# Softmax denominators: seven tiles summed onto the same 224 columns, and the logarithm read from that bank

## The chip, the cores and the metric

The kernel runs on one core of one Trainium2 chip. The metric is the device time in microseconds (us) of one execution; a figure for a kernel is the median of its runs.

## The reference, cut to what matters

Inputs are q, k and v of shape 8 x 12 x 448 x 64 (batch, heads, sequence, head width), two gains of 64, and the weights w_in (768 x 2048) and w_out (2048 x 768) of a two-layer network.

```python
q_n, k_n = rmsnorm(q, g_q), rmsnorm(k, g_k)
scores = scale * q_n @ k_n.transpose(0, 1, 3, 2)
attn = exp(scores - max)
attn = attn / (sum(attn, axis=-1) + 1e-09)     # the sum is the denominator of this case
x = (attn @ v) reshaped to (8 * 448, 768)
h = x @ w_in
out = maximum(0.01 * h, h) @ w_out             # leaky relu between the two products
```

## The kernel before

**Units.** The attention is cut into 24 units, numbered u = 0 to 23. A unit is four heads of one batch element, held as two pairs: index `a` picks the pair and index `r` the head of the pair (`r` is the upper or lower half of the 128 partitions of the scores). The 448 sequence positions are seven tiles of 64 (`NS` = 7). Three units make one batch element, and each batch element then passes through the two-layer network, whose pieces stand in a queue.

**One unit.** For each of the seven key tiles TensorE makes the scores (`score`, L195) into a slot: two banks of PSUM, the tile `sT`. ScalarE writes `et` = exp(score + shift) in 16 bits (`ex`, L214). The shift comes from the first tile: VectorE takes its maximum (L232) and spreads it on a diagonal (L234), TensorE transposes it (`shift_mm`, L244), VectorE reduces it again (L245) and makes the bias `eb` (L253). There are two slots, so the scores of the coming tiles wait until the exponentials of earlier ones have read their slot.

**Close of a unit.** When the scores of the first tile of unit u have been issued (step d = 0 of four), unit u-1 is closed. For units 4 to 22 (`narrow`) this is done as follows, in this order:

- `pv_slot`: 28 matmuls (L341) give exp times v in the other slot, without the division; each is a 64 x 64 piece of TensorE, and four of them run beside each other.
- `zcol`: the sums of exp, the denominators, go to a bank `zc` (L283). The stationary operand `onesr` has 32 columns of ones and zeros, so that each matmul uses 128 rows and 32 columns of the array. Four such matmuls, for the four combinations of the half `y` of the sequence and the pair `a`, use the four strips of 32 columns beside each other. The kernel before takes two key tiles in one matmul where it can: three groups of 448 columns (two tiles side by side) and one group of 224 columns (the seventh tile, added onto the first half). That makes 16 matmuls, and the bank then holds two halves of 224 columns.
- `shift_mm` for unit u, then `pv_out` (ScalarE copies the undivided result from the slot to `x32`, L295).
- `zcol_sum`: VectorE adds the two halves of `zc` into `zs` (L300), after which the bank can be used again.

Then the exponential of unit u's first tile is issued. Later, as a job between the pieces of the network, `zcol_inv` takes on ScalarE exp(-ln(zs)) (L305 and L306) and issues four DMAs on SP's queue that spread the reciprocals over the partitions (`rz`, L311). A later step on GpSimd or VectorE multiplies `x32` by `rz` into `xt` (L321), the input of the network.

**The order of the work.** All order is written by hand in the loop at L928 to L1006. `fill` takes pieces of the network out of the queue and puts one waiting job after each piece. `moe1` is six matmuls of 448 columns (`hps`, L363) and the leaky relu on ScalarE (L357). `moe2` and `seven` are the second product (L404, L445). In the last batch elements `late1` gives the first product in other pieces (L565, with L575 and L578 behind them).

**Banks.** PSUM has two slots of two banks and four further banks in rotation, called `aux`. `zc`, `hps` and the accumulators of the second product come out of these four, so that the fourth request after `zc` gets the bank of `zc`. From the late pieces on the four banks stand in a list (`held`): `aux` takes the first and `drop` appends.

For the last unit, u = 23, the job `zcol_inv` of unit 22 is issued at step d = 1 and not at d = 0.

Of the kernel before, what the change touches and what calls it, by code (L numbers as in the profile page):

```python
# [10 lines left out]
AF = mybir.ActivationFunctionType  # L11
ALU = mybir.AluOpType
AXL = mybir.AxisListType
# [5 lines left out]
def kernel(  # L19
# [11 lines left out]
    nc = tc.nc  # L31

    B, H, S, D = q.shape
    QH = 4
    NS = 7
# [21 lines left out]
    def aux(shape, dtype, name):  # L57
        if held:
            return held[0].pop(0)
        return psum.tile(shape, dtype, tag="aux", bufs=4, name=name)  # L60
# [6 lines left out]
    def drop(bank):  # L67
        if held:
            held[0].append(bank)
# [5 lines left out]
    onesr = cst.tile([P, 32], FP16)  # L75
# [47 lines left out]
    def load_v(u):  # L123
        nc.gpsimd.dma_start(vts[u % NV].rearrange("p a t d -> p a (t d)"), rows(v, u))  # L124
# [73 lines left out]
    def qk(u, steps):  # L198
        st[u]["sT"] = []
        for t in steps:  # L200
            sT = slot()
            score(u, t, (sT[:, 0], sT[:, 1]))
            st[u]["sT"].append((t, sT))

    def ex(u):
        s = st[u]
        if "et" not in s:
            s["et"] = epool.tile([P, NS, 2, S], FP16, tag="et", name="et")
        for t, sT in s["sT"]:
            if isinstance(sT, list):  # L210
                for a in range(2):
                    nc.scalar.activation(s["et"][:, t, a], sT[a][:, 0:S], AF.Exp, bias=s["eb"], scale=1.0)
            else:
                nc.scalar.activation(s["et"][:, t], sT[:, :, 0:S], AF.Exp, bias=s["eb"], scale=1.0)  # L214
# [6 lines left out]
    def shift_max(u):  # L221
        s = st[u]
        sT = s["sT"][0][1]
        if isinstance(sT, list):
            pm2 = small.tile([P, 2], FP32, tag="pm2", name="pm2")
            for a in range(2):
                nc.vector.tensor_reduce(pm2[:, a:a + 1], sT[a][:, 0:S], axis=AXL.X, op=ALU.max)
            s["spare"] = sT[0]
            nc.vector.tensor_reduce(s["spare"][:, 511:512], pm2, axis=AXL.X, op=ALU.max)
        else:  # L230
            s["spare"] = sT[:, 0]
            nc.vector.tensor_reduce(s["spare"][:, 511:512], sT[:, :, 0:S], axis=AXL.XY, op=ALU.max)  # L232
        s["dg"] = small.tile([P, P], FP16, tag="dg", name="dg")
        nc.vector.tensor_tensor(s["dg"], ident16, s["spare"][:, 511:512].broadcast_to([P, P]), op=ALU.mult)  # L234
# [20 lines left out]
    def gate(u):  # L255
        nc.gpsimd.tensor_copy(gate_t, buf(u, "n16")[:, 1, NS - 1, 1, D - 1:D])
# [11 lines left out]
    def zsum_slot(u):  # L268
        s = st[u]
        s["zslot"] = slot()  # L270
        s["zt"] = [s["zslot"][:, r] for r in range(2)]
        zsum(u)

    HS = S // 2

    def zcol(u):
        s = st[u]
        s["zc"] = aux([P, 512], FP32, "zc")
        for i, (t, n) in enumerate(((0, 2), (NS - 1, 1), (2, 2), (4, 2))):
            for y in range(2):  # L280
                for a in range(2):
                    c = 32 * (2 * y + a)
                    nc.tensor.matmul(s["zc"][c:c + 32, 0:n * HS].rearrange("p (k x) -> p k x", k=n), onesr,  # L283
                                     s["et"][:, t:t + n, a, HS * y:HS * y + HS], start=(i == 0), stop=(i == 3))

    def pv_slot(u):
        s = st[u]
        s["pslot"] = slot()
        s["pv"] = [s["pslot"][:, r] for r in range(2)]
        pv(u)  # L290

    def pv_out(u):
        s = st[u]
        s["x32"] = zpool.tile([P, 2, S], FP32, tag="x32", name="x32")
        nc.scalar.copy(s["x32"], s["pslot"][:, :, 0:S])  # L295

    def zcol_sum(u):
        s = st[u]
        s["zs"] = zpool.tile([P, HS], FP32, tag="zs", name="zs")
        nc.vector.tensor_reduce(s["zs"], s["zc"][:, 0:S].rearrange("p (k x) -> p x k", k=2), axis=AXL.X, op=ALU.add)  # L300
        drop(s["zc"])

    def zcol_inv(u):
        s = st[u]
        nc.scalar.activation(s["zs"], s["zs"], AF.Ln)  # L305
        nc.scalar.activation(s["zs"], s["zs"], AF.Exp, bias=0.0, scale=-1.0)  # L306
        s["rz"] = zpool.tile([P, 2, S], FP32, tag="rz", name="rz")
        for r in range(2):
            for y in range(2):
                src = s["zs"][64 * y + r:64 * y + 64:2, None, :]  # L310
                nc.sync.dma_start(s["rz"][:, r, HS * y:HS * y + HS], src.broadcast_to([32, 4, HS]))  # L311

    def xmul_sb(u):
        xmul_pool(u, nc.vector)
# [382 lines left out]
    def narrow(u):  # L697
        return 4 <= u < NU - 1

    def fed(u, d):  # L700
        return u % NQ == 0 and d == 3
# [43 lines left out]
    with tc.manual_schedule():  # L745
# [182 lines left out]
        for u in range(3, NU):  # L928
            for d in range(4):
                if d > 0 or u > 3:  # L930
                    qk(u, STEPS[d])
                    if d == 0:
                        shift_max(u)
                        if u == 6:
                            xmul_sb(u - 2)
                        if narrow(u - 1):
                            pv_slot(u - 1)
                            zcol(u - 1)
                            shift_mm(u)
                            pv_out(u - 1)  # L940
                            zcol_sum(u - 1)
                        else:
                            zsum_slot(u - 1)
                            pv(u - 1)
                            shift_mm(u)
                            zinv(u - 1)
                    ex(u)
                jobs = []

                def job(fn, *args):  # L950
                    jobs.append(lambda: fn(*args))

                if d == 0:
                    if u == 3:
                        prep_norm(4)
                        gate(4)
                    elif narrow(u - 1):
                        if u < NU - 1:
                            job(zcol_inv, u - 1)
                    else:  # L960
                        xmul(u - 1)
                    if u + 4 < NU:
                        job(load, u + 4)
                    if u + 3 < NU:
                        load_v(u + 3)
                    if u < 6:
                        prep_sqp(u + 3)
                if d == 1 and narrow(u - 1) and not 5 <= u < 8 and u < NU - 1:
                    xmul_pool(u - 1)
                if u == NU - 1:  # L970
                    if d == 1:
                        job(zcol_inv, u - 1)
                    if d == 2:
                        xmul_pool(u - 1)
                if fed(u, d) and u > 3:
                    push(u // NQ - 1)
                if (u, d) in ((3, 1), (4, 0)):
                    for ti in range(2):
                        prep_tr(u + 1, ti, VV)
                if d == 1 and 5 <= u < NU - 1:  # L980
                    job(prep_g, u + 1)
                if u + 2 < NU:
                    if d == 1:
                        for ti in range(2):
                            job(prep_ssq, u + 2, ALL, (ti,))
                    if d == 2:
                        job(prep_rinv, u + 2)
                        for ti in range(2):
                            job(prep_norm, u + 2, ALL, (ti,))
                        if u > 3:  # L990
                            job(prep_trd, u + 2)
                if d == 1 and 4 <= u < 8:
                    job(weight_sum, u - 4, 0)
                if d == 0 and 5 <= u < 9:
                    job(weight_sum, u - 5, 1)
                if d == 2 and 6 <= u < 8:
                    job(xmul_sb, u - 1)
                if u == NU - 2 and d == 0:
                    for n, tile_ in ((1, (raws, "rq", 3)), (2, (raws, "rk", 3)), (3, None), (4, (prep_p, "sq", 3))):
                        job(win_sum, n, 1, tile_)  # L1000
                    for n in (3, 1, 2, 4):
                        job(x_sum, LATE, n)
                if d == 3 and 6 <= u < NU - 3:
                    for ti in range(2):
                        job(prep_sq, u + 3, ALL, (ti,))
                fill(u, d, jobs)  # L1006
# [4 lines left out]
        for i, ns in enumerate(((3, 1), (2, 4))):  # L1011
            c, fn = queue[i]
# [33 lines left out]
```

## Time and profile before

| What | Value |
|---|---|
| Median of 5 runs | 421.41 us (420.49 to 423.85) |
| Time of the profiled execution | 422.01 us |
| Its span, first to last instruction | 420.2 us |
| Around the span | 1.81 us |
| Mean granted TensorE clock | 0.990 of full speed |
| TensorE, matmuls (PE) | 404.6 us busy, 96% of the span |
| TensorE, weight loads (PEld) | 217.8 us, 52% |
| VectorE (DVE) | 279.9 us, 67% |
| ScalarE (ACT) | 304.8 us, 73% |
| GpSimd (POOL) | 82.9 us, 20% |
| `zc` matmuls L283, 19 units | 304 matmuls |
| `zs` sum on VectorE L300 | 19 instructions, 622 to 624 ns each |
| ln L305 and exp L306 on ScalarE | 19 each, 395 and 390 ns |

PE is TensorE's matmuls and PEld its weight loads, which lie beside the matmuls. A matmul's duration in the profile contains its way through the array, so that neighbouring matmuls overlap; how long a row of matmuls holds TensorE is read from the distance of their starts, or from the chain of waits.

### The profile page before, as it was taken

How to read it: one execution, taken by the hardware profiler on the slowest of the kernel's cores; microseconds unless marked ns; L12 is line 12 of the kernel's file. 1: busy time of each engine (PE TensorE's matmuls, PEld its weight loads, DVE VectorE, ACT ScalarE, POOL GpSimd, SP SyncE). 2: the span in 40 equal slices, each digit the busy share in tenths (PEclk: the TensorE clock that was granted, in tenths of full speed). 3: DMA queues.
4: the chain of work that ended last, by engine and by line, in shares of the span. 5: the costliest groups of instructions: out<-in, count | busy, mean ns of one | idle time of the engine just before them, and what ended most of it. 6: DMA issues, size and time to landing. Idle time of an engine off the chain costs nothing.

```text
span 420.2 us, 9148 instructions
## 1 busy us (share of the span) xinstructions
PE 404.6 (96%) x3731; PEld 217.8 (52%) x3731; DVE 279.9 (67%) x459; ACT 304.8 (73%) x474; POOL 82.9 (20%) x75
## 2 busy tenths in 40 slices
PE   7977999999999999999999999999999999999995
PEld 6544444444445544454445544454445547558853
DVE  5788666898569746567349856478349888627762
ACT  5999878867987779867986779967986757653600
POOL 0958421300020111220111112121101101010000
PEclk9699999999999999999999999999999999999999
DMA  7999995989664796687565797577562460032023
GB/s 255 219 251 257 239 250 111 194 156 213 172 153 73 217 211 118 171 159 175 157 125 118 194 192 161 144 143 192 162 112 45 119 148 17 2 83 76 2 53 98
DMA packets 71949, 62.39 MB, mean 148 GB/s; under 512 B 36324, under 2 KB 67044, under 8 KB 71908
## 3 DMA queue, kind: packets, MB, share of 16 engines
q1 hardware_dynamic: 61312, 49.62, 46.6%
q0 software_dynamic: 10272, 11.80, 17.9%
q8 instruction: 29, 0.48, 0.4%
q10 hardware_dynamic: 324, 0.39, 0.3%
q14 instruction: 12, 0.10, 0.1%
HBM read 45.61 MB, written 11.01 MB: 135 GB/s over the span
## 4 chain that ended last, share of the span: by engine, by line
PE 82%; ACT 8%; DVE 6%; issue 1%; DMA 1%; SPq 0%; DVEq 0%; ACTq 0%
PE hps L363 27%; PE sT L195 8%; PE sT L341 6%; PE ma L445 5%; PE md L445 5%; PE mc L445 5%; ACT et L214 5%; PE bank L445 5%; PE bank L565 4%; PE op L404 3%; PE zc L283 3%; PE mb L445 3%; DVE n L167 2%; PE sT L445 2%; DMA rk<-in_k_dram 1%
## 5 line engine op out<-in xcount | busy, mean ns | idle before, releaser
L214 ACT ACTIVATE et<-sT,eb 128x896 f16<-128x896 f32 x166 | 159.5, 1009 | 17.9 <-PE sT L195 16.3
L363 PE MATMUL hps<-xt,win 128*128 128x448 f16 x600 | 120.8, 353 | 0.2 <-DVE xt L350 0.2
L363 PEld LDWEIGHTS <-win 128*128 128x128 f16 x612 | 56.8, 98 | 58.2 <-issue 9.6
L321 POOL TENSOR_TENSOR xt<-x,rz 128x896 f16<-128x896 f32 x16 | 33.2, 2076 | 148.7 <-DMA rz<-zs 117.8
L167 DVE TENSOR_TENSOR n<-rq,rinv 128x896 f16<-128x896 f32 (+2 forms) x25 | 26.8, 1075 | 51.5 <-ACT rinv L161 48.7
L357 ACT ACTIVATE gt<-hps 128x448 f16<-128x448 f32 x100 | 52.4, 549 | 5.4 <-PE hps L363 5.1
L195 PE MATMUL sT<-qkT 64*64 64x448 f16 x664 | 53.2, 368 | 3.0 <-ACT et L214 2.1
L155 DVE TENSOR_REDUCE ssq<-sq 128x14 f32<-128x896 f32 (+2 forms) x49 | 50.4, 1058 | 1.7 <-ACT sq L144 1.7
L445 PEld LDWEIGHTS <-sa 128*128 128x128 f16 x352 | 32.8, 98 | 26.3 <-issue 6.1
L295 ACT COPY x<-sT 128x896 f32<-128x896 f32 x19 | 17.2, 906 | 36.1 <-DVE sT L245 36.1
L124 POOL DMA_DIRECT2D vt<-in_v_dram x24 | 18.2, 758 | 114.4 <-PE sT L341 106.9
L445 PEld LDWEIGHTS <-gt 128*128 128x128 f16 x264 | 25.2, 98 | 18.7 <-issue 2.1
L195 PEld LDWEIGHTS <-qkT 64*64 64x64 f16 x672 | 15.1, 105 | 36.9 <-issue 33.7
L341 PE MATMUL sT<-et,vt 64*64 64x448 f16 x532 | 28.5, 349 | 0.3
L404 PE MATMUL op<-wout,gt 128*128 128x384 f16 x160 | 28.4, 327 | 0.0
L232 DVE TENSOR_REDUCE sT<-sT 128x1 f32<-128x896 f32 x22 | 24.1, 1094 | 4.6 <-PE sT L195 4.5
L341 PEld LDWEIGHTS <-vt 64*64 64x64 f16 x672 | 20.7, 107 | 11.3 <-issue 1.7
L167 DVE TENSOR_TENSOR n<-rk,rinv 128x896 f16<-128x896 f32 (+2 forms) x26 | 26.1, 1011 | 0.0
L404 PEld LDWEIGHTS <-gt 128*128 128x128 f16 x192 | 17.6, 98 | 14.0 <-issue 3.0
L445 PE MATMUL ma<-wout,gt 128*128 128x384 f16 x128 | 23.5, 326 | 0.0
L426 DVE TENSOR_TENSOR sa<-gt 128x512 f16<-128x512 f16 (+1 forms) x15 | 8.2, 543 | 16.0 <-ACT gt L357 12.1
L144 ACT ACTIVATE sq<-rq 128x896 f32<-128x896 f32 (+2 forms) x18 | 16.3, 913 | 1.2 <-DMA rq<-in_q_dram 1.2
(136 smaller groups left out, 524.6 us busy)
## 6 DMA issues: line engine op xcount, KB each, us to landing
rq<-in_q_dram SPq DMA_DIRECT2D x24, 448.0 KB, 4.1
rk<-in_k_dram SPq DMA_DIRECT2D x24, 448.0 KB, 5.5
out_dram<-ost SPq DMA_DIRECT2D x52, 192.0 KB, 2.9
rz<-zs SPq DMA_DIRECT2D x76, 112.0 KB, 2.3
vt<-in_v_dram POOLq DMA_DIRECT2D x24, 224.0 KB, 5.4
win<-in_moe_w_in_dram POOLq DMA_DIRECT2D x8, 384.0 KB, 12.8
wout<-in_moe_w_out_dram POOLq DMA_DIRECT2D x2, 1536.0 KB, 26.1
out_dram<-ost SPq DMA_DIRECT2D x4, 96.0 KB, 2.1
```

The costliest lines, as they stand in the source:

```text
L124: nc.gpsimd.dma_start(vts[u % NV].rearrange("p a t d -> p a (t d)"), rows(v, u))
L155: nc.vector.tensor_reduce(buf(u, "ssq")[:, ti, :, c[0]:c[1]], buf(u, f"sq{ti}")[:, :, c[0]:c[1]], axis=AXL.X, op=ALU.add)
L167: nc.vector.tensor_tensor(buf(u, "n16")[:, ti, c[0]:c[1]].rearrange("p s a d -> p a s d"), src[:, :, c[0]:c[1]], buf(u, "rinv")[:, ti, :, ...
L195: nc.tensor.matmul(banks[a][64 * r:64 * r + 64, 0:S].rearrange("p (t x) -> p t x", t=NS), kT(u, r, a, t), qT(u, r, a), start=True, stop=True)
L214: nc.scalar.activation(s["et"][:, t], sT[:, :, 0:S], AF.Exp, bias=s["eb"], scale=1.0)
L232: nc.vector.tensor_reduce(s["spare"][:, 511:512], sT[:, :, 0:S], axis=AXL.XY, op=ALU.max)
L321: eng.tensor_tensor(xts[b][:, g], s["x32"], s["rz"], op=ALU.mult)
L341: nc.tensor.matmul(s["pv"][r][64 * a:64 * a + 64, 0:S], vts[u % NV][64 * r:64 * r + 64, a, t], s["et"][64 * r:64 * r + 64, t, a], start=(t ...
L357: nc.scalar.activation(dst, src, AF.Prelu, bias=0.0, scale=1.0, alpha=0.01)
L363: nc.tensor.matmul(hps[:, 0:S], win16[:, kt // 2, kt % 2, ts(ft, P)], xt[:, kt // 2, kt % 2], start=(kt == 0), stop=(kt == KT - 1))
L404: nc.tensor.matmul(op2[:, 0:HC], gt[:, ft, ds(col(t), P)], wout16[:, ft, ds(HC * half, HC)], start=(ft == 0), stop=(ft == FT - 1))
L445: nc.tensor.matmul(bank[:, 0:HC], a[:, f], b[:, f], start=(first and f == 0), stop=(f == HF - 1), skip_group_check=not first)
```

## The change

The seven key tiles are now seven groups of four matmuls with 224 columns each, all accumulated onto the same 224 columns of the bank, so that 28 matmuls replace 16. The sum of two halves on VectorE is gone. ScalarE's logarithm, which was the first instruction of the later job `zcol_inv`, reads the bank itself; it is issued right after the exponential of the first tile of unit u, in all of the 19 units. The exponential of minus the logarithm and the four DMAs stay where they were.

```diff
     def zcol(u):
         s = st[u]
         s["zc"] = aux([P, 512], FP32, "zc")
-        for i, (t, n) in enumerate(((0, 2), (NS - 1, 1), (2, 2), (4, 2))):
+        for t in range(NS):
             for y in range(2):
                 for a in range(2):
                     c = 32 * (2 * y + a)
-                    nc.tensor.matmul(s["zc"][c:c + 32, 0:n * HS].rearrange("p (k x) -> p k x", k=n), onesr,
-                                     s["et"][:, t:t + n, a, HS * y:HS * y + HS], start=(i == 0), stop=(i == 3))
+                    nc.tensor.matmul(s["zc"][c:c + 32, 0:HS], onesr, s["et"][:, t, a, HS * y:HS * y + HS],
+                                     start=(t == 0), stop=(t == NS - 1))
...
-    def zcol_sum(u):
+    def zcol_ln(u):
         s = st[u]
         s["zs"] = zpool.tile([P, HS], FP32, tag="zs", name="zs")
-        nc.vector.tensor_reduce(s["zs"], s["zc"][:, 0:S].rearrange("p (k x) -> p x k", k=2), axis=AXL.X, op=ALU.add)
+        nc.scalar.activation(s["zs"], s["zc"][:, 0:HS], AF.Ln)
         drop(s["zc"])
 
     def zcol_inv(u):
         s = st[u]
-        nc.scalar.activation(s["zs"], s["zs"], AF.Ln)
         nc.scalar.activation(s["zs"], s["zs"], AF.Exp, bias=0.0, scale=-1.0)
...
                             zcol(u - 1)
                             shift_mm(u)
                             pv_out(u - 1)
-                            zcol_sum(u - 1)
                         else:
...
                     ex(u)
+                    if d == 0 and narrow(u - 1):
+                        zcol_ln(u - 1)
```

## The prediction

> **What bounds the kernel now.** I read the page first (busy shares, then the chain that ended last), then that chain in order of time, then one unit by timeline, then the groups of instructions for durations.
>
> The page:
>
> ```profile
> PE 404.6 (96%) x3731; PEld 217.8 (52%) x3731; DVE 279.9 (67%) x459; ACT 304.8 (73%) x474; POOL 82.9 (20%) x75
> ...
> PE 82%; ACT 8%; DVE 6%; issue 1%; DMA 1%; SPq 0%; DVEq 0%; ACTq 0%
> ```
>
> TensorE's matmuls are busy for 96% of the span and make 82% of the chain. The VectorE sum that the change removes (L300) isn't among the chain's named lines, while the `zc` matmuls (L283) are, with 3%. The chain of waits around one close of a unit (start, us, what):
>
> ```profile
> 209.24 0.31 PE sT L195 x4
> 209.55 1.32 PE sT L341 x28
> 210.88 0.78 PE zc L283 x16
> 211.66 0.17 PE sT L244 x2
> 211.82 3.40 PE hps L363 x18
> ```
>
> TensorE passes from one row to the next without a break; the 0.78 us of `zc` lie wholly on the path, 19 times (14.8 us). What VectorE and ScalarE do meanwhile, from the timeline of the same unit:
>
> ```profile
> 212.25 0.91 ACT L295 COPY x<-sT 128x896 f32<-128x896 f32 x1 [1.42 <-DVE sT L245]
> 212.37 0.62 DVE L300 TENSOR_REDUCE zs<-zc 128x224 f32<-128x448 f32 x1
> ...
> 213.05 1.01 ACT L214 ACTIVATE et<-sT,eb 128x896 f16<-128x896 f32 x1
> ...
> 213.95 0.55 ACT L357 ACTIVATE gt<-hps 128x448 f16<-128x448 f32 x1
> 214.38 0.40 ACT L305 ACTIVATE zs<-zs 128x224 f32<-128x224 f32 x1
> 214.81 0.39 ACT L306 ACTIVATE zs<-zs 128x224 f32<-128x224 f32 x1
> ```
>
> The sum is done at 212.99, 1.4 us before the logarithm begins: ScalarE does not wait for it. One place is different, the first step of the last unit, in the chain of waits:
>
> ```profile
> 352.91 3.56 PE bank L565 x36
> ...
> 359.47 0.91 ACT x L295
> 360.38 0.91 ACT et L214
> 361.29 0.90 ACT gt L575 x2
> 362.19 0.43 ACT gt L357
> 362.62 0.44 ACT gt L575
> 363.06 0.05 issue
> 363.11 0.50 PE bank L404 x2
> ```
>
> Here TensorE has run out of work and waits until ScalarE has passed its list. From 363.11 on the chain is TensorE's again until 396.85.
>
> **TensorE's part.** The columns that stream through each strip stay the same: 3 x 448 + 224 = 1568 before, 7 x 224 = 1568 after. What grows is the number of starts. In the trace's records of single matmuls, the four matmuls of a `zc` group start 2 to 4 ns apart and run beside each other; in the unit at 210.81 the groups start at 0, 201, 297 and 486 ns, and the next instruction (L244) at 780. So a group of 448 holds TensorE for 189 ns, the group of 224 for 96, the first group 12 more than its columns, and after the last group there are 96 ns beyond its columns. All 19 units show the same within 2 ns, apart from two closes where L244 came 15 and 38 ns later. Seven groups of 224 thus take (96 + 12) + 5 x 96 + (96 + 96) = 780 ns by the 96, as before by rounding; by the two widths, (189 - 96) / 224 = 0.415 ns for a column and 3 ns fixed for a group, the three further groups cost 9 ns. I take 9 ns, x 19 = +0.17 us. Each group needs new loads of the stationary operand, even though it is the same: a load takes 97 ns (the weight-load row of L283), just as long as a group of 224, and it starts when the previous group does. The row that shows such a rhythm sustained is L565: matmuls of 224 columns, each with its own load of 98 ns, start 95 to 96 ns apart over a whole stretch (36 in 3.56 us, of which the first has a switch ahead of it). What L565 does not show is four loads and four matmuls in each 96 ns; for `zc` itself that is shown once per unit, between its second and third group, not six times in a row. Bounds: below, no gain, since the columns are unchanged; above, the 28 pairs of L341 that take 1.32 us, 47 ns for each load and matmul, which would make the 28 of `zc` about 1.32 us and, with the 0.11 of switching to and from their strips (12 + 96 above), 1.43 us, +0.65 x 19 = +12.4 us. I take the 96 ns, since that row is the same instruction in the same array strips.
>
> The Trainium skill, "TensorEngine Tiling (Array Packing)", section "Instruction Overhead", speaks against the change: it gives each matmul about 60 cycles of overhead on this chip and advises against cutting a dimension that is already small. Read as a cost of each further matmul, with a cycle as the 0.415 ns of a column, 12 x 60 cycles would be an estimated 0.3 us for each unit and 5.7 us in all, that is 427.1 us. The starts 2 to 4 ns apart speak against that reading.
>
> **VectorE's part.** 19 sums of 622 ns go: 11.8 us of 279.9. In the unit shown the next VectorE work (L151 at 212.91, L155 at 213.27) comes 0.6 us earlier and then VectorE waits for `rinv` (7.2 us idle before L167 at 205.66 in the unit ahead). In the two heavy units, at 74.38 and 87.51, VectorE stands idle right after, 1.58 us before L408 at 76.57 and 0.97 before the one at 89.10, so the gain ends in idle time. I take 0.
>
> **ScalarE's part.** The logarithm reads PSUM now. Logarithms from PSUM take 908 ns (L327, 896 columns) and 535 (L331, 448), the exponentials from SBUF that follow them 951 (L328) and 577 (L332); from SBUF the two functions cost alike (395 in L305, 390 in L306). So PSUM saves some 42 ns, and the 395 become some 350. In the five places from 78 us on where TensorE waits for an exponential (below), this can give 0.04 each, -0.1 to -0.2 us; I take -0.1. The new wait is for the last `zc` matmul, over by 211.58, and for the last unit's DMAs out of `zs`, which VectorE waited for until now. Behind the logarithm stand the leaky relu L357, L306 and the next exponentials; the relu moves back by 0.43 us (start of L305 to start of L306). Nobody waits for that here: the bank it frees is wanted four requests later. The bank of `zc` comes free about 1.3 to 1.4 us later, at some 214.3 instead of 212.99. The fourth request after it begins at 215.66 in this unit, and at 340.37 + 3 x 1.14 = 343.8 in the densest one (24 `hps` matmuls in a row), where the logarithm would end at 342.9. So 0.9 us are left at the least, and I take 0; without that cover it would cost the overlap, up to 0.5 us a unit.
>
> At the last unit the cover is missing. There the logarithm was at 365.77, behind the scores of step 1; now it stands between the exponential and the four relus (L575, L575, L357, L575) for which TensorE waits until 363.11. That adds its 0.43 us to the chain, +0.4 us, not given back before the end, since TensorE is the bound from there. SP's queue keeps its order; the DMAs follow L306, which starts no later by more than 0.1 us.
>
> **Sum.** +0.17 + 0.4 - 0.1 = +0.5 us. The profiled execution, 420.2 of span and 1.81 around it, goes from 422.01 to 422.5. It lies 0.6 above the median of the runs, so the forecast for the median is 421.41 + 0.5 = 421.9 us. A measurement of this kernel can tell about 0.5%, 2.1 us (419.3 to 423.5), from no change; the forecast is "the same".
>
> **Rival 1, slower: the groups of 224 don't keep their rhythm.** Twice as many loads and matmuls must be fed in the same time, 24 ns for a pair. The mechanism would be one of supply or of loading: each group starts when its four loads are through, and six such starts follow each other where now only one does. It decides from the point at which a unit loses 0.11 us (2.1 / 19), that is 96 + 18 = 114 ns a group or 28.5 ns a pair. For it: the two full-width matmuls of L244 start 28 to 40 ns apart with their own loads though they have only 64 columns, and a load of 97 ns leaves no slack at 96. Against it: the third group of every close starts on time. At 33 ns a pair, inside L244's spread, a group takes 132, a unit loses 6 x 36 = 0.22 us, and the sum is 421.9 + 4.1 = 426.0 us. Chance 0.26.
>
> **Rival 2, faster: TensorE's breaks close.** From 71 us on the records show breaks in TensorE of 0.29 us at 78.4, 0.58 at 91.0, 0.28 at each of 175.9, 240.6 and 271.7 (all before scores or products that wait for exponentials), 0.13 at 85.9, 0.39 at 362.6 and 0.37 at 398.1. An engine freed of 11.8 us could bring the exponentials forward. The first five sum to 1.7 us. For it: they hang on ScalarE, whose bias comes from VectorE. Against it: the sum stands behind the bias (L253 at 212.19, L300 after it), so the bias of the same unit doesn't move. If all five closed: 421.41 + 0.17 + 0.4 - 1.7 = 420.3 us; with half, 421.1. Chance 0.13, of which 0.05 for more than the trace lets me see, over 0.5%.
>
> **How the numbers follow.** The forecast's own case has 0.61: 421.9, by its terms 421.3 to 422.6. Slower by over 0.5% is most of rival 1, 0.25; faster by over 0.5% is 0.05; the remaining 0.70 is within. The range goes down to 420.2, where rival 2 would end, and up to 425.6, which takes in rival 1 up to about 32 ns a pair; what lies beyond on both sides is below 2 in 10.
>
> **What would show it.** Right: in the chain, `zc` L283 x28 with 0.78 to 0.80 us; group starts 96 ns apart; L300 gone; the logarithm at some 350 ns; relus 0.4 us later after the first exponential and TensorE's break before L404 in the last unit about 0.8 us instead of 0.39; VectorE at some 268 us busy with more idle time. Wrong: `zc` at 0.9 us or more in the chain (rival 1), TensorE's breaks before L195 and L341 gone (rival 2), or matmuls of L363 or L445 that wait for the logarithm's bank.

## The result, and the profile after

The changed kernel takes 421.94 us (median; 421.03 to 422.64) beside 421.35 for the kernel before: a ratio of 1.0014, 95% interval 1.0008 to 1.0019. The forecast was 421.9 and "the same". The direction and the total came out; the runs show below that the parts of the sum did not all do so.

The profiled execution takes 422.02 us, 420.2 of it span. Its page, with the chain's shares:

```profile
PE 404.0 (96%) x3959; PEld 222.8 (53%) x3959; DVE 270.2 (64%) x440; ACT 303.5 (72%) x474; POOL 83.0 (20%) x75
...
PE 80%; ACT 9%; DVE 6%; issue 2%; DMA 1%; SPq 0%; DVEq 0%; ACTq 0%
```

VectorE has lost 9.7 us of work and the span has lost none. TensorE has 228 matmuls more and is no busier. In the chain, ScalarE and "issue" have each gained a point. The close of the same unit in the chain of waits (start, us, what):

```profile
208.99 0.31 PE sT L195 x4
209.30 1.32 PE sT L340 x28
210.62 0.79 PE zc L283 x28
211.41 0.17 PE sT L244 x2
```

28 matmuls take what 16 took. In the records of single matmuls the seven groups start at 0, 107, 203, 299, 395, 490 and 586 ns, and L244 at 787 instead of 780. Every unit but the two named in the prediction (821 and 792) is within 786 to 788.

VectorE and ScalarE beside it, from the timeline:

```profile
212.00 0.91 ACT L295 COPY x<-sT 128x896 f32<-128x896 f32 x1 [1.43 <-DVE sT L245]
212.02 0.44 DVE L151 TENSOR_SCALAR qkT<-qkT,gcol 128x896 f16<-128x896 f16 x1
...
212.80 1.01 ACT L214 ACTIVATE et<-sT,eb 128x896 f16<-128x896 f32 x1
213.70 0.36 ACT L300 ACTIVATE zs<-zc 128x224 f32<-128x224 f32 x1
213.94 0.56 ACT L356 ACTIVATE gt<-hps 128x448 f16<-128x448 f32 x1
214.36 0.41 ACT L305 ACTIVATE zs<-zs 128x224 f32<-128x224 f32 x1
```

L300 is now the logarithm. It takes 358 ns, and the relu behind it starts 0.24 us after it, not 0.43. The last unit, in the chain:

```profile
359.46 0.64 DVE v L577
360.09 0.99 ACT et L214
361.08 0.24 ACT zs L300
361.33 0.90 ACT gt L574 x2
362.23 0.43 ACT gt L356
362.66 0.44 ACT gt L574
363.10 0.05 issue
363.15 0.50 PE bank L403 x2
```

The logarithm stands in this chain with 0.24 us, and TensorE's break before L403 has grown from 0.39 to 0.63 us, as the prediction said, though by less.

One thing is new that no step of the prediction has: a break of 0.52 us in TensorE at 143.95. A break is here the distance between the starts of two neighbouring matmuls less the time that the columns of the first take (0.415 ns each), and it is given at the start of the first; the figure in a line's brackets counts from the first one's recorded end and is smaller. The timeline of the changed kernel there:

```profile
141.09 2.07 POOL L320 TENSOR_TENSOR xt<-x,rz 128x896 f16<-128x896 f32 x1 [8.91 <-DMA rz<-zs]
...
141.98 2.13 DVE L167 TENSOR_TENSOR n<-rq,rinv 128x896 f16<-128x896 f32 x1 [0.31 <-ACT rinv L161]
...
144.03 0.55 DVE L451 TENSOR_TENSOR ost<-md,ost 128x384 f32<-128x384 f32 x1
...
144.63 1.46 PE L444 MATMUL md<-tw,gt 128*128 128x384 f16 x8 [0.35 <-DVE ost L451]
```

And of the kernel before, which reaches this place 0.8 us later because its start-up took longer:

```profile
140.35 2.07 POOL L321 TENSOR_TENSOR xt<-x,rz 128x896 f16<-128x896 f32 x1 [7.37 <-DMA rz<-zs]
...
142.78 1.09 DVE L167 TENSOR_TENSOR n<-rq,rinv 128x896 f16<-128x896 f32 x1 [0.32 <-ACT rinv L161]
```

Read it backwards. TensorE waits for VectorE's addition L451, which frees a bank. L451 stands behind L167, which took 2.13 us instead of 1.09. L167 ran beside GpSimd's multiply; before, the multiply was over 0.36 us before L167 began. The multiply is late because rz is: it starts 6.06 us after the first rz DMA was issued, in 12 of the other 15 units from 118 us on, 4.3 to 4.4. In the trace's records of DMA packets a packet of 16,384 bytes on the instruction queue (q8, 29 packets before and 31 after; TensorE's 7480 and 7936 instruction records are 29.2 and 31.0 times 256) starts 3.3 us after that issue and lasts 1.34 us, and the last rz packet ends at 5.3 us instead of 3.9. In the kernel before, no such packet falls into this unit's transfer. Two fall into later transfers there (0.5 us after the rz issue at 231.41 and 1.7 after that at 246.51), without a break of TensorE.

The Trainium skill states both halves: "Runtime: NRT & Kernel Launch", section "Instruction fetch mechanics", that instructions are refilled in blocks of 16 KiB, 256 instructions, at a cost that is mostly hidden; and "SBUF — State Buffer", section "Who interferes with whom", that a VectorE instruction with two inputs in SBUF contends with a GpSimd instruction that reads SBUF. The 1.09 and 2.13 us fit the second. The size of the blocks fits the counts of q8; that the cost is mostly hidden does not hold for the transfer that a block meets here.

### The profile page after: what moved, and what is told of

It is laid out like the page before. It is cut to its first block, busy times and chain, and to the rows that moved or that the text cites. A ratio compares the mean times of both kernels' runs of the same rounds, so it can differ in the third digit from the quotient of the medians.

```text
span 420.2 us, 9568 instructions
## 1 busy us (share of the span) xinstructions
PE 404.0 (96%) x3959; PEld 222.8 (53%) x3959; DVE 270.2 (64%) x440; ACT 303.5 (72%) x474; POOL 83.0 (20%) x75
## 4 chain that ended last, share of the span: by engine, by line
PE 80%; ACT 9%; DVE 6%; issue 2%; DMA 1%; SPq 0%; DVEq 0%; ACTq 0%
PE hps L362 27%; PE sT L195 8%; ACT et L214 6%; PE sT L340 6%; PE ma L444 5%; PE bank L444 5%; PE md L444 5%; PE bank L564 4%; PE mc L444 4%; PE op L403 3%; PE zc L283 3%; PE mb L444 3%; DVE n L167 2%; PE sT L444 2%; DMA rk<-in_k_dram 1%
## 5 line engine op out<-in xcount | busy, mean ns | idle before, releaser
L167 DVE TENSOR_TENSOR n<-rq,rinv 128x896 f16<-128x896 f32 (+2 forms) x25 | 28.3, 1134 | 47.5 <-ACT rinv L161 44.8
L356 ACT ACTIVATE gt<-hps 128x448 f16<-128x448 f32 x100 | 53.9, 556 | 6.1 <-PE hps L362 5.4
L295 ACT COPY x<-sT 128x896 f32<-128x896 f32 x19 | 17.2, 906 | 36.9 <-DVE sT L245 36.9
L403 PE MATMUL op<-wout,gt 128*128 128x384 f16 x160 | 28.4, 327 | 0.0
L167 DVE TENSOR_TENSOR n<-rk,rinv 128x896 f16<-128x896 f32 (+2 forms) x26 | 26.1, 1011 | 0.0
L403 PEld LDWEIGHTS <-gt 128*128 128x128 f16 x192 | 17.6, 98 | 14.3 <-issue 3.0
```

Source lines behind the costliest of these rows:

```text
L167: nc.vector.tensor_tensor(buf(u, "n16")[:, ti, c[0]:c[1]].rearrange("p s a d -> p a s d"), src[:, :, c[0]:c[1]], buf(u, "rinv")[:, ti, :, ...
L356: nc.scalar.activation(dst, src, AF.Prelu, bias=0.0, scale=1.0, alpha=0.01)
L403: nc.tensor.matmul(op2[:, 0:HC], gt[:, ft, ds(col(t), P)], wout16[:, ft, ds(HC * half, HC)], start=(ft == 0), stop=(ft == FT - 1))
```

## The experiments

Theory after this reading: three costs, namely the groups (7 ns a unit, 0.13 us), the last unit's logarithm (0.24 us), and a meeting of fetch and rz (about 0.5 us) that belongs to no part of the change but to the number of TensorE instructions ahead of that place. Rivals: the logarithm costs in every unit; the longer instruction stream itself slows TensorE.

Ratios are to the kernel before on the same chip (420.95, 421.15 and 421.09 us in the three sets), with 95% intervals. The profiles' start-up differs by up to 1.7 us; so the table also gives the stretch from the first `zc` matmul to the end of the span, less that of the kernel before (347.30 us). It is one profile each. The breaks at 228, 162, 178, 179 and 323 lie between `zc` and L244, where every close has 0.10 already.

| Kernel | Median us | Ratio | Stretch | Breaks of TensorE that changed |
|---|---|---|---|---|
| changed, first measurement | 421.94 | 1.0014 (1.0008 to 1.0019) | +0.81 | 0.52 at 144; 0.63 at 362 |
| e0 changed, again | 422.03 | 1.0026 (1.0016 to 1.0036) | +0.68 | 0.38 at 144; 0.64 at 362 |
| e1 groups only | 421.54 | 1.0012 (1.0001 to 1.0023) | +0.65 | 0.53 at 144; 0.39 at 362 |
| e2 logarithm only | 421.28 | 1.0006 (0.9996 to 1.0016) | +0.18 | 0.64 at 361 |
| e3 last unit mended | 421.49 | 1.0012 (1.0001 to 1.0022) | +0.55 | 0.47 at 143; 0.39 at 362 |
| e4 groups of 112 | 423.23 | 1.0049 (1.0030 to 1.0067) | +1.14 | 0.14 at 145; 0.51 at 228; 0.64 at 363 |
| e5 logarithm late | 421.68 | 1.0015 (1.0002 to 1.0027) | +0.31 | 0.64 at 362 |
| e6 VectorE loaded | 421.79 | 1.0018 (1.0009 to 1.0027) | +0.86 | 0.39 at 162; 0.37 at 178; 0.63 at 362 |
| e7 changed, more warming instructions | 422.11 | 1.0024 (1.0014 to 1.0034) | +0.82 | 0.51 at 190; 0.64 at 363 |
| e8 before, more warming instructions | 421.43 | 1.0013 (1.0002 to 1.0024) | +0.38 | 0.52 at 179; 0.39 at 363 |
| e9 e7 and the copy on VectorE | 421.02 | 1.0000 (0.9990 to 1.0009) | +0.18 | 0.48 at 191; none at 362 |
| e10 before and the copy on VectorE | 420.50 | 0.9985 (0.9977 to 0.9994) | -0.37 | none at 362 |
| e11 changed, 32 instructions more | 421.57 | 1.0009 (0.9999 to 1.0019) | +0.55 | 0.35 at 323; 0.64 at 362 |

**The change again, and its parts.**

e0 is the changed kernel as it stands.

> The changed kernel once more, on the chip on which its parts are timed. Known: 421.94 us beside 421.35, a ratio of 1.0014. Theory (two costs): 7 groups instead of 4 cost 7 ns a unit on TensorE (0.13 us), and the logarithm in front of the last unit's relus lengthens TensorE's break before L403 by 0.24 us; together +0.4 us. In the first profile of the changed kernel there was also a break of 0.52 us at 143.95, where VectorE's L167 took 2.13 us instead of 1.09 beside a GpSimd multiply that had started 1.5 us late. If that break belongs to the change, it comes again at the same place; if it is chance in the landing of the rz DMAs, it is gone or elsewhere.

The break came again at the same place, 0.38 us at 143.86, with a fetch 3.3 us after the rz issue and L167 at 1.99 us. So it is not peculiar to one profile.

e1, the groups alone (remarks behind # are added, here and below):

```diff
-        nc.scalar.activation(s["zs"], s["zc"][:, 0:HS], AF.Ln)      # after ex(u)
+        nc.vector.tensor_copy(s["zs"], s["zc"][:, 0:HS])            # where zcol_sum was
...
     def zcol_inv(u):
+        nc.scalar.activation(s["zs"], s["zs"], AF.Ln)
```

> Half of the change: seven groups of 224 on the same columns, but VectorE copies the 224 columns out of the bank where it used to sum two halves, and the logarithm stays in the later job, from SBUF. The theory of two costs expects only the first: zc 787 ns instead of 780 a unit, the break before L403 back at 0.39 us, and before + 0.1 us (421.5). The rival that the whole difference lies in the feeding of TensorE with 456 more instructions expects before + 0.6.

The groups cost 787 ns a unit and the last break is back at 0.39, as expected. But the break at 144 came with the groups, without the moved logarithm, and the time is before + 0.5 us by the ratio, not + 0.1.

e2, the logarithm alone:

```diff
-        for t in range(NS):
+        for i, (t, n) in enumerate(((0, 2), (NS - 1, 1), (2, 2), (4, 2))):   # zcol of the kernel before
```

> The other half: the four groups of before (two halves in the bank), and the logarithm right after the first exponential, from the bank, reading only the first half. The second half is left out of the denominators, so that no VectorE sum is needed. The theory expects zc at 780 ns, the break before L403 at 0.63 us, and before + 0.25 us (421.6). The rival that the logarithm's move costs in every unit expects most of the 0.6 here; the rival that all lies in the feeding of TensorE expects before + 0.

zc at 780 ns, the last break at 0.64, no break at 144, before + 0.3 us. The interval holds no change too; the trace, though, shows the one expected cost and nothing in the other units. The rival that the logarithm costs in every unit falls.

e3, the last unit mended:

```diff
     def zcol_ln(u):
-        nc.scalar.activation(s["zs"], s["zc"][:, 0:HS], AF.Ln)
+        if u == NU - 2:
+            nc.vector.tensor_copy(s["zs"], s["zc"][:, 0:HS])       # and Ln again in zcol_inv for this unit
+        else:
+            nc.scalar.activation(s["zs"], s["zc"][:, 0:HS], AF.Ln)
```

> The changed kernel with the last unit mended: there VectorE copies the 224 columns out of the bank and the logarithm stands at step 1 again, as in the kernel before. The theory expects the break before L403 back at 0.39 us and 0.24 us less than the changed kernel (421.7, before + 0.15 to 0.35). If the break is not on the path that sets the end, the time stays at before + 0.6.

The break went back to 0.39 and the ratio fell from 1.0026 to 1.0012 beside e0 on the same chip, more than the 0.24 us of the break, within the intervals.

**Where the groups would lose their rhythm.** e4 cuts each group in two.

```diff
-        for t in range(NS):
+        for h in range(2):
+          for t in range(NS):
...
-                    nc.tensor.matmul(s["zc"][c:c + 32, 0:HS], onesr, s["et"][:, t, a, HS * y:HS * y + HS],
+                    x0 = HS * y + HQ * h                            # HQ = HS // 2
+                    nc.tensor.matmul(s["zc"][c:c + 32, HQ * h:HQ * h + HQ], onesr, s["et"][:, t, a, x0:x0 + HQ],
                                      start=(t == 0), stop=(t == NS - 1))
```

> The changed kernel with each group of 224 columns cut into two of 112: 14 groups, 56 matmuls and 56 loads a unit, the same 1568 columns. It looks for the point at which groups no longer keep their rhythm. By columns and 3 ns a group (the terms of the prediction), zc goes from 787 to some 808 ns, +0.4 us in all. If a group can't start before its own load of 97 ns is through, counted from the start of the group ahead (rival 1 of the prediction), 14 groups take about 1470 ns, +0.68 us a unit and +13 us in all. Anything between shows a limit in the supply of pairs: at 25 ns a pair 1.5 us as well, at 16 ns a pair 1.0. The phase of the fetches moves too, worth up to 0.5 us either way.

The close of a unit in its chain of waits:

```profile
209.78 1.32 PE sT L343 x28
211.10 0.80 PE zc L286 x56
```

56 matmuls and 56 loads take 805 ns from the first matmul to L244: by columns and 3 ns a group, and even a little below. A pair is fed every 12 ns or so, and a group starts about 50 ns after the one ahead though its load lasts 97. Rival 1 of the prediction was far from deciding. The time rose by 2.1 us against before, in four executions. In the profile the stretch grew by 1.14 us, and the groups (25 ns x 19 = 0.5), the last break (0.24) and two breaks behind late rz transfers (0.14, and 0.42 beyond what every close has) make about 1.3. The further 1.0 us of the medians is not located.

**The place of the logarithm and VectorE's relief.** In e5 the logarithm reads the bank from within the later job, in all units but the last.

```diff
+                    if d == 0 and narrow(u - 1) and u == NU - 1:
                         zcol_ln(u - 1)
...
     def zcol_inv(u):
+        if u < NU - 2:
+            zcol_ln(u)
```

> The changed kernel with the logarithm, still read from the bank, at its old place in the later job, behind the first relu, in all units but the last. The bank of zc is held some 0.4 us longer and the first relu is 0.4 us earlier. Theory: both are covered, same time as the changed kernel (before + 0.6 to 1.1), zc 787 ns, all breaks as there. If the place of the logarithm or the holding of the bank costs something in every unit, it moves by more than 0.4 us, up or down.

No new break, zc at 787 ns: holding the bank longer is covered. The break at 144 is missing here; the fetch came 3.9 us after the rz issue, when that transfer was through. Why it came 0.6 us later than in e0 with the same TensorE instructions stays open. The stretch is shorter than that of e0 by 0.37 us, as the missing break would have it. The ratio is not lower: 1.0015 beside 1.0014 and 1.0026. With intervals of 0.1% each way the medians can't confirm the price of the break, which is read from single profiles, and in how many of the other executions fetch and transfer meet is not known.

e6 gives VectorE its load back.

```diff
                             pv_out(u - 1)
+                            nc.vector.tensor_reduce(j, st[u - 1]["et"][:, 0, 0].rearrange("p (k x) -> p x k", k=2),
+                                                    axis=AXL.X, op=ALU.add)
```

> The changed kernel with VectorE loaded again: where the sum of two halves was, it reduces 448 elements of another tile to 224 (about 0.6 us, 19 times) for nothing. The prediction counted the relief of VectorE at 0: then the time is that of the changed kernel, before + 0.6 to 1.1. If the relief is worth something that the longer zc hides, this kernel is slower than the changed one by up to 1.7 us.

The same time as the changed kernel within the intervals (1.0018 beside 1.0026 and 1.0014), so the relief buys nothing that this comparison, good to about 0.1%, could see. It is not quite a clean test: the meeting at 144 is missing (fetch at 3.8 us), and in its place VectorE, with a L167 of 2.72 us at 157.6 beside GpSimd, came late twice (0.39 and 0.37 us of break, 0.29 and 0.28 of it new).

**The meeting of fetch and rz.** In e7 and e8 most of the 74 warming matmuls, which stand at the start and whose results nobody uses, are cut into two of half the width, which puts 136 TensorE instructions ahead of everything.

```diff
-            nc.tensor.matmul(bank[:, P:2 * P], onesp, onesp, start=True, stop=True)
+            for w in range(2 if x < split else 1):
+                c = P // 2 if x < split else P
+                nc.tensor.matmul(bank[:, P:P + c], onesp, onesp[:, 0:c], start=True, stop=True)
...
-        warm(32, wbank)
+        warm(32, wbank, 32)
...
-        warm(42, wbank)
+        warm(42, wbank, 36)
```

> The changed kernel, and 68 of the 74 matmuls that warm TensorE's clock at the start are cut into two of half the width: the same columns, 136 more TensorE instructions before anything else. Nothing of the change is touched. New theory: TensorE's instructions are fetched in pieces of 16 KB, 256 instructions each; in the changed kernel a fetch at 138.3 us falls into the rz transfer of one unit, rz lands 1.4 us later, GpSimd's multiply runs beside VectorE's L167, which then takes 2.1 us, and TensorE breaks off for 0.4 to 0.5 us at 143.9. With 136 instructions more the fetch comes some 7.6 us earlier, at about 131, before the transfer. Expected: the break at 143.9 gone, L167 there at 1.09 us, and 0.4 to 0.5 us less than the changed kernel (before + 0.4). If the break belongs to the new groups or the logarithm, it stays, and the time with it.

At 142.32 L167 takes 1.09 us again and the break is gone from there. But the time did not fall, because the break moved. The timeline of e7, three units later:

```profile
187.43 2.07 POOL L320 TENSOR_TENSOR xt<-x,rz 128x896 f16<-128x896 f32 x1 [8.92 <-DMA rz<-zs]
...
188.32 2.13 DVE L167 TENSOR_TENSOR n<-rq,rinv 128x896 f16<-128x896 f32 x1 [0.32 <-ACT rinv L161]
...
190.97 0.81 PE L444 MATMUL md<-tw,gt 128*128 128x384 f16 x4 [0.35 <-DVE ost L451]
```

A fetch now starts 3.2 us after the rz issue of this unit (181.36), and the same picture repeats: L167 at 2.13 us, a break of 0.51.

> The kernel before with the same cut of the warming matmuls, and no part of the change. The fetch that lay at 146.9 us comes to about 139, into the rz transfer that starts at 135.9. Theory of the fetches: rz of that unit lands about 1 us late, L167 there takes up to 2 us, a break of 0.3 to 0.5 us appears before a matmul of L445 near 144.7, and before + 0.3 to 0.5 us. If the break belongs to the change, nothing appears and the time is that of before.

Not at the place expected, since the fetch came 0.6 us after the issue instead of 3 (L167 there 1.34 us, no break). But two units on, in a kernel without any part of the change, the same chain:

```profile
172.27 2.07 POOL L321 TENSOR_TENSOR xt<-x,rz 128x896 f16<-128x896 f32 x1 [8.23 <-DMA rz<-zs]
173.52 1.76 DVE L167 TENSOR_TENSOR n<-rq,rinv 128x896 f16<-128x896 f32 x1 [4.96 <-ACT rinv L161]
...
179.00 0.29 DVE L234 TENSOR_TENSOR dg<-ident,sT 128x128 f16<-128x128 f16 x1
179.34 0.22 PE L244 MATMUL sT<-dg,onesp 128*128 128x64 f16 x2 [0.36 <-DVE dg L234]
```

The delay goes down VectorE's list, the diagonal `dg` is late, and TensorE breaks off for 0.52 us, 0.43 more than at other closes. The kernel before gets slower by 0.13% (0.02 to 0.24%) from instructions that do nothing. So such a break needs no part of the change; what the change did was to move a fetch. Nor does every long L167 cost TensorE time: one unit earlier, at 158.90, L167 took 2.13 us and no break followed.

e11 shifts by 32 instructions alone: `warm(32, wbank, 16)`.

> The changed kernel with only 16 of the warming matmuls cut in two: 32 TensorE instructions more, so that the fetch that lay at 138.3 comes some 1.8 us earlier, at 136.5, 1.5 us after the first rz transfer of its unit instead of 3.3. Theory of the fetches: rz is late by 0.7 us instead of 1.4, VectorE's L167 takes some 1.4 us instead of 2.1, no break appears at 143.9, none of the other fetches from 160 on falls at 2 to 4 us after an rz issue of a unit with little slack, and the time is 0.4 to 0.5 us less than the changed kernel (before + 0.4 to 0.6 on this chip). If the break belongs to the change, it stays.

The break at 143.9 is gone (L167 1.18 us) and the ratio is the lowest of the changed kernels that keep both of its parts and the last unit's order, 1.0009, though its interval overlaps theirs. One of e11's twelve executions took 1024 us; it is not in the ratio, and nothing recorded explains it. Another fetch came 0.3 us after an rz issue at 309.89, GpSimd started 0.9 us late, and L431 (0.85 us in the changed kernel) met it:

```profile
315.16 2.07 POOL L320 TENSOR_TENSOR xt<-x,rz 128x896 f16<-128x896 f32 x1 [8.41 <-DMA rz<-zs]
315.79 1.73 DVE L431 TENSOR_TENSOR sa<-gt 128x512 f16<-128x512 f16 x1
```

This gave a break of 0.35 us at 322.8, 0.25 of it new. The expectation that no other fetch would meet a transfer was wrong, and the places were forecast badly in all three runs: fetches were expected at 131, 139 and 136.5 us in e7, e8 and e11 and came at 132.4, 136.8 and 135.2.

All fourteen profiles together, with 266 rz transfers, show the two links of the chain. The last rz packet usually ends 3.9 us after the issue. In 47 transfers a fetch started within 3.4 us after the issue; all 47 ended late, by 0.2 to 1.7 us. In the 176 that had no fetch start from 2 us ahead of the issue to 3.4 behind it, none ended more than 0.24 late. And where L167 began more than 0.1 us before the end of GpSimd's multiply, 54 times, it ended 0.94 to 0.99 us after that multiply; behind the multiply's end it took 1.07 to 1.10 us.

**A version below both.** The last unit's break depends on ScalarE's list; e9 and e10 take the copy L295 of that unit off it.

```diff
-        nc.scalar.copy(s["x32"], s["pslot"][:, :, 0:S])
+        (nc.vector.tensor_copy if u == NU - 2 else nc.scalar.copy)(s["x32"], s["pslot"][:, :, 0:S])
...
-                            pv_out(u - 1)
+                            if u < NU - 1:
+                                pv_out(u - 1)
...
+                    if d == 0:                           # of u = 23; comes to stand behind L577 (L578 in e10)
+                        for _ in range(2):
+                            job(lambda: None)
+                        job(pv_out, u - 1)
```

> The changed kernel with the cut warming matmuls, and in the last unit the copy of the undivided result (L295) on VectorE, behind its addition L577, instead of on ScalarE ahead of the first exponential. ScalarE's list before TensorE's break at 362 then loses 0.9 us of copy. Expected: that break (0.64 us) gone, 0.6 us less than the changed kernel with the cut alone, which is before - 0.2 us: about the only way here to end below the kernel before. If the break is held by something else than ScalarE's list, it stays.

> The kernel before with the one edit of the last unit: the copy L295 on VectorE, behind the addition L578. The break of 0.39 us before L404 should go, so that before - 0.35 us remains, below both kernels; a little may stay, since VectorE's sum (0.62 us) still stands ahead of L578 there.

In e10's chain nothing stands between TensorE's rows any more:

```profile
360.03 0.57 PE bank L565 x6
360.61 1.34 PE bank L404 x8
361.94 0.50 PE sT L195 x8
```

By the ratios e9 gains 0.24% on e7, of which the break accounts for 0.64 us, 0.15%; the rest is within the intervals. e10 is 0.15% below the kernel before (420.50 us), the fastest version of this study.

## Why the prediction was right, and by how much its parts were

**TensorE's part: right.** 9 ns was taken, 7 measured; the case rested on the one group of 224 per unit that the trace already showed, and e4 shows that the limit lies below 50 ns a group. One reading was off: beyond the columns of the last group there are 105 ns, not 96 (it starts at 486, L244 at 780, and a group of 448 takes 189). With 105 the sum by the 96 gives 789 ns, so it agrees with the 9 ns that were taken and not with "as before".

**VectorE's part: right that the relief is worth 0**, as far as e6 can tell, and by the breaks at 78, 176, 240 and 272, which stand at 0.28 to 0.29 as before. Rival 2 falls.

**ScalarE's part: the size was off.** The logarithm takes 358 ns (350 taken), but where -0.1 us was counted only the break at 91 shrank, by 0.03. The bank that is held longer costs nothing, as reasoned (e5).

**The last unit: mechanism right, term mis-sized.** 0.43 us was taken from the distance of L305 to L306; 0.24 was measured. The exponential reads what the logarithm writes, and starts 0.03 us after the logarithm's end. The relu that follows now depends on nothing of it, and starts 0.12 us before that end; the distance of two independent ScalarE instructions would have been the row to take.

**The step that was missing:** "SP's queue keeps its order; the DMAs follow L306". That holds for the issue (L305 of the changed kernel, the old L306, even starts 0.17 to 0.19 us earlier, counted from the first `zc` matmul, in 11 of the 19 units). It says nothing of the landing. The 456 TensorE instructions more were priced by their streaming alone; they also move the times of all later fetches, and one fetch met the rz transfer of a unit where 0.4 us of slack separated GpSimd's multiply from L167. With it the sum of the profile is 0.13 + 0.24 + 0.52 - 0.03 = 0.86 us, beside 0.81 in the stretch and 0.59 between the medians. That the forecast of +0.5 came so close is luck: its own three terms, as measured, make 0.34, and a term of 0.4 to 0.5 was left out. The mechanisms that it named were there; one that it did not name gave the larger part of the rise in the profile.

## What to carry to other kernels

Matmuls that run beside each other in strips of the array, cut into more and shorter ones, cost almost nothing here as long as the columns were the same (7 ns a close at 224 columns, 25 at 112), but look for what the extra instructions do elsewhere: the times of the instruction fetches move, and a transfer with little slack can be hit. When a difference of a tenth of a per cent is to be explained, list the breaks of the bounding engine in both traces; here three lines of such a list and the groups account for it. Price an instruction that is put into a chain by the distance to an independent successor, not to one that reads its result.

## What the runs showed of the hardware

- A fetch of 16,384 bytes of instructions lasts 0.9 to 2.4 us as one packet; where it started 3.2 to 3.3 us after the first of the four rz DMAs, the last rz packet came 0.9 to 1.7 us late in all eleven such transfers of these profiles; with a start at 0.3 to 2.7 us it came 0.3 to 1.4 late, and at 3.7 or more on time. A fetch that started up to 2 us ahead of the issue left 36 of 43 transfers within 0.13 us of the usual time; the other seven came 0.25 to 1.0 late.
- L167, VectorE's multiply of two inputs in SBUF, takes 2.13 us instead of 1.09 when GpSimd's multiply is 0.9 us under way, and ends 0.95 us after GpSimd does, as in all 54 such meetings (0.94 to 0.99): it seems to stand until GpSimd is nearly through. GpSimd's own time stays at 2.07.
- Four strips of 32 columns of the array, each with its own load, take a new group every 50 ns at 112 columns, half the recorded 97 ns of a load.
